# A load moved to another queue, two dummy products fewer and a new order of transposes, in the first ten microseconds of a linear-attention and SwiGLU mix

## Chip, cores, metric

One core of one Trainium2 chip. The metric is device time in microseconds (us) per execution; lower is better. "PE" is the matrix engine (TensorE), "DVE" VectorE, "ACT" ScalarE, "POOL" GpSimd, "SP" the sync engine, which here only issues loads and stores.

## The reference, cut to what matters

```python
# x: 2048 tokens of 512; all bf16
g = sigmoid((x * gate_w).sum(-1, keepdims=True))
q, k, v = split(x @ wqkv)                    # 32 heads of 16
phi = lambda t: where(t > 0, t + 1, exp(t)) + 1e-6
a = (phi(q) @ (phi(k).T @ v) / (phi(q) @ sum(phi(k)))) @ wo     # per head
b = (silu(x @ w1) * (x @ w3)) @ w2
out = g * a + (1 - g) * b
```

Only the start matters here: the keys `k = x @ wk` of the first four tiles of 128 tokens and their `phi`.

## The kernel before

A key product needs x transposed. For later tokens the load does that (DMA_TRANSPOSE in the trace; the first three landed 5.5 to 6.0 us after their issue); for the first four tiles PE transposes (four 128x128 transposes a tile into PSUM, then two copies back into `xT`, half 0 on DVE, half 1 on ACT). While nothing has landed yet, PE runs dummy products (`emit_warm`). PE's instructions are put in the order written (the kernel sets `tc.manual_schedule` for PE); on the other engines the scheduler chooses the order.

```python
    dq = nc.sync
    dq.dma_start(out=x_sb[:, 0:1, :], in_=x_r[:, 0:1, :])          # x tile 0
    for i in range(2):
        kcs = slice(2 * i, 2 * i + 2)
        nc.scalar.dma_start(out=wk_sb[:, kcs, :], in_=wqkv_r[:, kcs, D : 2 * D])
    dq.dma_start(out=x_sb[:, 1:2, :], in_=x_r[:, 1:2, :])          # x tile 1
    dq.dma_start(out=x_sb[:, 2:TPB, :], in_=x_r[:, 2:TPB, :])      # x tiles 2 and 3
    # ... (cut: all other loads, on the sync queue)
    def phi(dst, ps):                       # exp on ACT, then two operations on DVE
        e_ins = nc.scalar.activation(out=e[:], in_=ps, func=ACT.Exp)
        nc.vector.tensor_scalar(out=em[:], in0=e[:], scalar1=1.0, scalar2=1e-6, op0=ALU.min, op1=ALU.add)
        nc.vector.scalar_tensor_tensor(out=dst, in0=ps, scalar=0.0, in1=em[:], op0=ALU.max, op1=ALU.add)
    # ...
    emit_warm(6)
    def emit_xT(t):
        for h in range(2):
            # ... (cut: two transposes into PSUM)
            if h == 0:
                nc.vector.tensor_copy(out=xT_t, in_=xTp[:])
            else:
                nc.scalar.activation(out=xT_t, in_=xTp[:], func=ACT.Copy)
    def emit_k_phi(k_ps, t):
        phi(pk_sb[:, t, :], k_ps[:])
        if t == 0:
            nc.gpsimd.tensor_copy(pks[:], pk_sb[:, t, :])      # the "cast" on GpSimd
        else:
            nc.gpsimd.tensor_add(pks[:], pks[:], pk_sb[:, t, :])
    # ...
    emit_xT(0)
    emit_warm(2)
    emit_k_mm(k0[0], 0, 0); emit_k_mm(k0[0], 0, 1)
    emit_xT(1)
    emit_k_mm(k0[0], 0, 2); emit_k_mm(k0[0], 0, 3)
    emit_k_phi(k0[0], 0)
    emit_xT(2)
    for t in range(1, TPB):
        for kc in range(KC):
            emit_k_mm(k0[t], t, kc)
        emit_k_phi(k0[t], t)
        if t == 1:
            emit_xT(3)
    # ... then XP products (x^T phi(k)) alternate with the key products of tile 4 on
```

## Time and profile before

| | before |
|---|---|
| time, median of 3 (range) | 180.97 us (180.84 to 181.03) |
| the profiled execution | 181.62 us, span 179.9 us |
| PE busy | 98% of the span |
| first key product / first XP product | 4.63 / 9.67 us |
| clock step (first record of the full clock in the trace) | 6.49 us |

The profiled execution was 0.6 us slower than the timed ones. From the page of the kernel before: the span, busy time of the engines, and the shares of the chain of waits that ended last.

```profile
span 179.9 us, 2484 instructions
...
PE 176.0 (98%) x892; PEld 84.7 (47%) x892; DVE 118.9 (66%) x205; ACT 66.7 (37%) x126; POOL 61.2 (34%) x69
...
PE 96%; DVE 2%; issue 0%; DVEq 0%
```

The timeline of PE in the kernel before: start, length, engine, line, operation, count (an idle time, where there is one, stands in brackets with what ended it). The end of a PE row is modelled and runs over the start of the next; read starts.

```profile
0.84 2.72 PE L158 MATMUL warm<-const-bfloat16-1.0 128*128 128x512 bf16 x6 [0.84 <-PEq L466]
3.35 0.63 PE L169 MATMUL xTp<-ident,x_sb 128*128 128x128 bf16 x4
3.78 1.06 PE L158 MATMUL warm<-const-bfloat16-1.0 128*128 128x512 bf16 x2
4.63 1.06 PE L179 MATMUL k<-wk_sb,xT 128*128 128x512 bf16 x2
5.49 0.63 PE L169 MATMUL xTp<-ident,x_sb 128*128 128x128 bf16 x4
5.91 0.88 PE L179 MATMUL k<-wk_sb,xT 128*128 128x512 bf16 x2
6.63 0.39 PE L169 MATMUL xTp<-ident,x_sb 128*128 128x128 bf16 x4
6.86 1.03 PE L179 MATMUL k<-wk_sb,xT 128*128 128x512 bf16 x4
7.72 0.39 PE L169 MATMUL xTp<-ident,x_sb 128*128 128x128 bf16 x4
7.94 1.89 PE L179 MATMUL k<-wk_sb,xT 128*128 128x512 bf16 x8
9.67 0.38 PE L199 MATMUL XP<-pk_sb,x_sb 128*128 128x512 bf16 x1
```

There is no hole from 0.84 us on. Two dummies start at 3.78 and 4.21, two key products at 4.63 and 5.06: 0.427 us apart. That is the stream time of a product before the clock step, the time from its start to the start of the next when nothing is awaited. After the clock step eight key products take 1.73 us (7.94 to 9.67), 0.216 us each; a transpose takes 0.107 and 0.056 us.

The timeline of DVE in the kernel before, in the same stretch (its first row left out):

```profile
6.95 0.29 DVE L174 COPY xT<-xTp 128x256 bf16<-128x256 bf16 x1 [0.71 <-PE xTp L169]
7.46 0.29 DVE L139 TENSOR_SCALAR phi_m<-phi_e 128x512 bf16<-128x512 bf16 x1 [0.23 <-ACT phi_e L137]
7.79 0.69 DVE L142 SCALAR_TENSOR_TENSOR pk_sb<-k,phi_m 128x512 bf16<-128x512 f32 x1
8.40 0.28 DVE L174 COPY xT<-xTp 128x256 bf16<-128x256 bf16 x1
8.59 0.71 DVE L139 TENSOR_SCALAR phi_m<-phi_e 128x512 bf16<-128x512 bf16 x1
```

GpSimd in the kernel before, the same view:

```profile
8.54 0.61 POOL L187 CAST pks<-pk_sb 128x512 f32<-128x512 bf16 x1 [5.56 <-DVE pk_sb L142]
```

L174 is the copy of a transposed half tile, L139 the first and L142 the second DVE step of phi. The copy of tile 2 (6.95) comes ahead of the first phi step of tile 0 (7.46). The phi step of tile 1 (8.59) took 0.71 us instead of 0.29, beside GpSimd's cast (8.54 to 9.15).

### The profile page before, as it was taken

The page shows a single profiled execution, that of the slowest core. Times are in us where ns is not written, and L with a number is a line of the kernel's source. Part 1 is how long each engine was busy: PE and PEld are TensorE (multiplying, and loading weights), DVE is VectorE, ACT ScalarE, POOL GpSimd, SP SyncE. Part 2 cuts the span into 40 slices and gives each one's busy share as a digit, 9 for nine tenths or more (in the row PEclk, how much of TensorE's full clock was granted, in tenths as well). Part 3 has the DMA queues.
Part 4 walks back from the last instruction along what each step waited for, and adds up shares of the span by engine and source line. Part 5 has one row for each costly group of instructions (what it writes and reads, how often), then busy time and mean ns, then how long its engine had stood idle before and what let it go on. Part 6 is the DMA issues. An engine that isn't in the chain of part 4 may idle for free.

```text
span 179.9 us, 2484 instructions
## 1 busy us (share of the span) xinstructions
PE 176.0 (98%) x892; PEld 84.7 (47%) x892; DVE 118.9 (66%) x205; ACT 66.7 (37%) x126; POOL 61.2 (34%) x69
## 2 busy tenths in 40 slices
PE   8999999999999999999999999999999999999993
PEld 3544444474444545444445454444545444444462
DVE  1497868596998937398777374987764669776000
ACT  4443322476623324243323343333443333331221
POOL 5177665645544323254003232620032327100000
PEclk9999999999999999999999999999999999999999
DMA  6999999901005010105000101240001013300011
GB/s 191 256 253 213 287 343 378 293 13 27 9 0 99 19 47 29 44 29 113 3 4 0 44 29 44 58 89 5 0 7 47 26 55 68 63 0 0 29 51 42
DMA packets 28285, 14.88 MB, mean 83 GB/s; under 512 B 19600, under 2 KB 27248, under 8 KB 28272
## 3 DMA queue, kind: packets, MB, share of 16 engines
q1 hardware_dynamic: 27728, 14.20, 29.3%
q10 hardware_dynamic: 544, 0.52, 0.9%
q8 instruction: 7, 0.11, 0.3%
q14 instruction: 6, 0.05, 0.1%
HBM read 8.42 MB, written 2.10 MB: 58 GB/s over the span
## 4 chain that ended last, share of the span: by engine, by line
PE 96%; DVE 2%; issue 0%; DVEq 0%
PE o_ps L345 19%; PE gate_ps L302 18%; PE up_ps L308 18%; PE XP L199 8%; PE o_ps L336 8%; PE q_ps L212 8%; PE k_ps L179 6%; PE r_ps L236 3%; PE k L179 2%; PE warm L158 2%; PE o_ps L340 2%; DVE hT L318 1%; PE xTp L169 1%; DVE gs L315 1%; PE kvT_ps L406 0%; PE W_ps L433 0%
## 5 line engine op out<-in xcount | busy, mean ns | idle before, releaser
L302 PE MATMUL gate_ps<-xT,w_sb 128*128 128x512 bf16 x160 | 41.1, 379 | 0.0
L308 PE MATMUL up_ps<-xT,w_sb 128*128 128x512 bf16 x160 | 41.1, 379 | 0.0
L220 POOL TENSOR_TENSOR qz<-pq,z_sb 128x512 f32<-128x512 bf16 x16 | 18.5, 1165 | 60.6 <-DVE pq L142 58.7
L313 ACT ACTIVATE th<-gate_ps 128x512 bf16<-128x512 f32 x40 | 23.9, 597 | 38.4 <-PE gate_ps L302 38.0
L345 PE MATMUL o_ps<-w_sb,hT 128*128 128x512 bf16 (+2 forms) x180 | 37.5, 355 | 0.0
L315 DVE SCALAR_TENSOR_TENSOR gs<-th,gate_ps 128x512 bf16<-128x512 bf16 x40 | 27.3, 683 | 6.1 <-ACT th L313 5.8
L318 DVE TENSOR_TENSOR hT<-up_ps,gs 128x512 bf16<-128x512 f32 x40 | 27.6, 691 | 3.7
L139 DVE TENSOR_SCALAR phi_m<-phi_e 128x512 bf16<-128x512 bf16 x32 | 14.9, 466 | 19.6 <-ACT phi_e L137 19.6
L345 PEld LDWEIGHTS <-hT 128*128 128x128 bf16 x180 | 16.8, 97 | 17.9
L308 PEld LDWEIGHTS <-w_sb 128*128 128x128 bf16 x160 | 15.7, 98 | 18.9 <-issue 0.2
L302 PEld LDWEIGHTS <-w_sb 128*128 128x128 bf16 x160 | 15.6, 98 | 18.8 <-issue 0.3
L350 ACT ACTIVATE o_out<-o_ps,omg 128x512 bf16<-128x512 f32 (+2 forms) x17 | 11.1, 656 | 30.4 <-PE o_ps L345 30.4
L285 POOL TENSOR_TENSOR pqn<-pq,rden 128x512 bf16<-128x512 bf16 x16 | 16.6, 1055 | 14.0 <-DVE rden L278 11.7
L189 POOL TENSOR_TENSOR pks<-pks,pk_sb 128x512 f32<-128x512 f32 x15 | 17.3, 1153 | 8.9 <-DVE pk_sb L142 8.4
L223 DVE TENSOR_REDUCE den<-qz 128x32 f32<-128x512 f32 x16 | 11.0, 686 | 8.9 <-POOL qz L220 8.9
L336 PE MATMUL o_ps<-W_sb,pqT 128*128 128x512 bf16 (+2 forms) x72 | 16.8, 355 | 0.0
L212 PE MATMUL q_ps<-wq_sb,xT 128*128 128x512 bf16 x64 | 16.3, 379 | 0.0
L199 PE MATMUL XP<-pk_sb,x_sb 128*128 128x512 bf16 x64 | 16.2, 379 | 0.0
L137 ACT ACTIVATE phi_e<-k_ps 128x512 bf16<-128x512 f32 x12 | 7.2, 597 | 15.4 <-PE k_ps L179 15.4
L179 PE MATMUL k_ps<-wk_sb,xT 128*128 128x512 bf16 x48 | 12.3, 379 | 0.0
L137 ACT ACTIVATE phi_e<-q_ps 128x512 bf16<-128x512 f32 x16 | 9.6, 597 | 7.0 <-PE q_ps L212 5.8
L142 DVE SCALAR_TENSOR_TENSOR pq<-q_ps,phi_m 128x512 bf16<-128x512 f32 x16 | 11.1, 691 | 0.5
(59 smaller groups left out, 121.4 us busy)
## 6 DMA issues: line engine op xcount, KB each, us to landing
w_sb<-in_B_w_dram SPq DMA_DIRECT2D x3, 1280.0 KB, 11.4
out_dram<-o_out SPq DMA_DIRECT2D x15, 128.0 KB, 1.7
x_sb<-in_A_x_dram SPq DMA_DIRECT2D x3, 512.0 KB, 4.5
wk_sb<-in_A_wqkv_dram ACTq DMA_DIRECT2D x2, 256.0 KB, 3.4
wq_sb<-in_A_wqkv_dram SPq DMA_DIRECT2D x1, 512.0 KB, 5.4
wv_sb<-in_A_wqkv_dram SPq DMA_DIRECT2D x1, 512.0 KB, 6.2
wo_sb<-in_A_wo_dram SPq DMA_DIRECT2D x1, 512.0 KB, 12.4
x_sb<-in_A_x_dram SPq DMA_DIRECT2D x2, 128.0 KB, 2.7
```

Of the source, the lines that this page charges most:

```text
L179: nc.tensor.matmul(k_ps[:], lhsT=xT[:, kc, t * P : (t + 1) * P], rhs=wk_sb[:, kc, :], start=(kc == 0), stop=(kc == KC - 1),)
L189: nc.gpsimd.tensor_add(pks[:], pks[:], pk_sb[:, t, :])
L199: nc.tensor.matmul(XP_ps[dc][:], lhsT=x_sb[:, t, dc * P : (dc + 1) * P], rhs=pk_sb[:, t, :], start=(t == 0), stop=(t == NT - 1),)
L212: nc.tensor.matmul(q_ps[:], lhsT=xT[:, kc, ts_tok], rhs=wq_sb[:, kc, :], start=(kc == 0), stop=(kc == KC - 1),)
L220: nc.gpsimd.tensor_tensor(out=qz[:], in0=st[tb, "pq"][:, tt, :], in1=z_sb[:], op=ALU.mult)
L302: nc.tensor.matmul(gate_ps[:], lhsT=w1_sb[:, kc, fsl], rhs=xT[:, kc, tok_sl], start=(kc == 0), stop=(kc == KC - 1),)
L308: nc.tensor.matmul(up_ps[:], lhsT=w3_sb[:, kc, fsl], rhs=xT[:, kc, tok_sl], start=(kc == 0), stop=(kc == KC - 1),)
L313: nc.scalar.activation(out=th[:], in_=gate_ps[:], func=ACT.Tanh, scale=0.5)
L315: nc.vector.scalar_tensor_tensor(out=gs[:], in0=th[:], scalar=1.0, in1=gate_ps[:], op0=ALU.add, op1=ALU.mult)
L318: nc.vector.tensor_tensor(out=st[tb, "hT"][:, fc, :], in0=up_ps[:], in1=gs[:], op=ALU.mult)
L336: nc.tensor.matmul(o_ps[:], lhsT=st[tb, "pqT"][:, c, tsl], rhs=W_sb[:, c, a:b], start=(c == 0), stop=False,)
L345: nc.tensor.matmul(o_ps[:], lhsT=st[tb, "hT"][:, fc, tsl], rhs=w2_sb[:, fc, a:b], start=False, stop=(fc == FC - 1),)
```

## The change

Its intent: bring the second half of wk in earlier, take out dummy products that seemed too many, and put each later group of transposes between the second and third product of the key tile before it, so that the copies have time.

```diff
-    for i in range(2):
-        kcs = slice(2 * i, 2 * i + 2)
-        nc.scalar.dma_start(out=wk_sb[:, kcs, :], in_=wqkv_r[:, kcs, D : 2 * D])
+    nc.scalar.dma_start(out=wk_sb[:, 0:2, :], in_=wqkv_r[:, 0:2, D : 2 * D])
+    dq.dma_start(out=wk_sb[:, 2:4, :], in_=wqkv_r[:, 2:4, D : 2 * D])
     dq.dma_start(out=x_sb[:, 1:2, :], in_=x_r[:, 1:2, :])
@@
-    emit_warm(6)
+    emit_warm(5)
@@
     emit_xT(0)
-    emit_warm(2)
-    (first key tile, transposes of tile 2, loop over the other tiles: as above)
+    emit_warm(1)
+    for t in range(TPB):
         for kc in range(KC):
+            if kc == KC // 2 and t + 1 < TPB:
+                emit_xT(t + 1)
             emit_k_mm(k0[t], t, kc)
         emit_k_phi(k0[t], t)
-        if t == 1:
-            emit_xT(3)
```

(The removed lines in brackets are cut; the kernel before has them above.) What the diff doesn't say: the scheduler also turned DVE's order round. After, the first phi step of tile 0 stands ahead of the copy of tile 2, and that of tile 1 ahead of the copy of tile 3.

More of the change, by code (lines that the diff above doesn't have):

```diff
@@ L364 @@
     emit_xT(0)
-    emit_warm(2)
-    emit_k_mm(k0[0], 0, 0)
-    emit_k_mm(k0[0], 0, 1)
-    emit_xT(1)
-    emit_k_mm(k0[0], 0, 2)
-    emit_k_mm(k0[0], 0, 3)
-    emit_k_phi(k0[0], 0)
-    emit_xT(2)
-    for t in range(1, TPB):
+    emit_warm(1)
+    for t in range(TPB):
         for kc in range(KC):
+            if kc == KC // 2 and t + 1 < TPB:
+                emit_xT(t + 1)
             emit_k_mm(k0[t], t, kc)
         emit_k_phi(k0[t], t)
-        if t == 1:
-            emit_xT(3)
     XP_ps = [psX.tile([P, D], FP32, tag=f"XP{dc}", name=f"XP{dc}") for dc in range(KC)]
```

## The prediction

> What bounds the kernel. The page gives PE 98% busy in a span of 179.9 us; 96% of the chain that ended last is PE. In the timeline PE runs back to back from the first dummy product at 0.84 us; after 6.9 us I find only about 0.4 us of PE gaps, none of them a wait for a load. So only the first 10 us, and the number of PE instructions in them, can move the time, and a shift of the first XP product (L199, at 9.67 us) should reach the end almost unchanged.
>
> The granted clock rises at 6.49 us. Before it 128x512 products follow each other every 427 ns and transposes every 107 ns; after it every 216 and 55 ns. [...]I assume that the step stays near 6.5 us.
>
> What changes.
> 1. One dummy fewer in front. x tile 0 lands at 3.21 us; its weight load starts at 3.25, the first transpose at 3.35, exactly 427 ns after the sixth dummy. The load held it as much as the dummy did: gain 0 to 0.07 us, and a hole of about 0.4 us in PE.
> 2. One dummy fewer behind. The first key product moves from 4.63 to about 4.2 us (it then waits for the DVE copy of xT, which ends at 4.10, not for wk). That is 427 ns of slow clock, but the clock step doesn't move with it: what is really won is one product at the fast clock, about 0.22 us.
> 3. Loads. In the trace they land: wk first half 3.85, x tile 1 4.21, wk second half 4.97, x tiles 2-3 5.88 us. On the other queue the second half should land at about 4.4 (needed at 5.5 now), x tile 1 at 4.6 to 4.9 (needed at 5.05), x tiles 2-3 near 5.9 (needed at 6.8). No new wait; also nothing that was waited for before.
> 4. The order on DVE changes, by the instruction orders: before, the copy of xT tile 2 stood ahead of phi_m of k0; now phi_m of k0 stands ahead of it, and phi_m of k1 ahead of the copy of tile 3. That phi_m waits for k0's last product and ACT's exp: last product at about 5.91, ends 6.54, exp (0.60) to 7.17, phi_m (0.29) to 7.49, copy (0.28) to about 7.73, weight load, product k2 at about 7.83. PE would be ready at 7.50: a new wait of about 0.33 us. The same at tile 3: about 0.06 us; if GpSimd's cast, which coincides with a phi_m of 0.71 instead of 0.29 us in the trace, gets in first, 0.5 us.
>
> Sum: -0.24 + 0.33 + 0.06, about +0.1 us: the first XP product at about 9.8 us instead of 9.67. All of it lies on the critical path.
>
> Predicted: 181.1 us, range 180.6 to 181.7. Faster by over 2%: 0.005; within 2%: 0.99; slower by over 2%: 0.005.
>
> What would show it: first key product at 4.2 us; no PE wait for x or wk; the first k2 product waiting 0.2 to 0.5 us for DVE's xT copy, which follows phi_m of k0; clock step near 6.5 us; first XP product at 9.7 to 9.9; from there the same lengths as before.
>
> What would make it wrong: the clock step moving ([...]an earlier step gains); x tile 1 landing after 5.1; the copies not waiting behind phi_m, then 180.7; phi_m of k1 delayed by GpSimd, then 181.6.

Two passages are cut from it, both on what moves the clock step. -0.24 + 0.33 + 0.06 = +0.15 us, which the prediction rounds to about +0.1 us.

## The result

| | before | after |
|---|---|---|
| time, median (range) | 181.03 us (180.84 to 181.74), 6 runs | 181.88 us (181.26 to 182.11), 6 runs |
| profiled execution: time, span | 181.62, 179.9 us | 181.69, 180.0 us |
| clock step | 6.49 us | 4.16 us |
| first key product / first XP product | 4.63 / 9.67 us | 4.34 / 9.86 us |
| first XP product to the end | 170.24 us | 170.10 us |

The ratio is 1.0033 (95% interval 1.0009 to 1.0058): slower by about 0.6 us. A ratio is the mean time of one kernel's runs over that of the other's of the same rounds, so not quite the ratio of the medians. A second set of the same two kernels gave 1.0001 (0.9980 to 1.0021), see below.

From the page of the kernel after, the lines that answer to those of before:

```profile
span 180.0 us, 2480 instructions
...
PE 174.9 (97%) x890; PEld 83.4 (46%) x890; DVE 118.7 (66%) x205; ACT 66.8 (37%) x126; POOL 61.2 (34%) x69
...
PE 93%; DVE 3%; DMA 2%; SPq 0%; ACT 0%; issue 0%; DVEq 0%
```

The timeline of PE after:

```profile
0.84 2.29 PE L157 MATMUL warm<-const-bfloat16-1.0 128*128 128x512 bf16 x5 [0.84 <-PEq L458]
3.56 0.61 PE L168 MATMUL xTp<-ident,x_sb 128*128 128x128 bf16 x4 [0.42 <-DMA x_sb<-in_A_x_dram]
3.96 0.48 PE L157 MATMUL warm<-const-bfloat16-1.0 128*128 128x512 bf16 x1
4.34 0.60 PE L178 MATMUL k<-wk_sb,xT 128*128 128x512 bf16 x2
5.32 0.40 PE L168 MATMUL xTp<-ident,x_sb 128*128 128x128 bf16 x4 [0.38 <-DMA x_sb<-in_A_x_dram]
5.56 1.04 PE L178 MATMUL k<-wk_sb,xT 128*128 128x512 bf16 x4
6.57 0.40 PE L168 MATMUL xTp<-ident,x_sb 128*128 128x128 bf16 x4
6.80 1.17 PE L178 MATMUL k<-wk_sb,xT 128*128 128x512 bf16 x4
7.81 0.39 PE L168 MATMUL xTp<-ident,x_sb 128*128 128x128 bf16 x4
8.03 0.59 PE L178 MATMUL k<-wk_sb,xT 128*128 128x512 bf16 x2
8.99 1.04 PE L178 MATMUL k<-wk_sb,xT 128*128 128x512 bf16 x4 [0.36 <-DVE xT L173]
9.86 0.38 PE L198 MATMUL XP<-pk_sb,x_sb 128*128 128x512 bf16 x1
```

The clock had stepped up at 4.16 us, 2.3 us earlier than in the trace before, and still the first XP product started later. PE waited for x tile 0 (row at 3.56), for x tile 1 (5.32), and for a DVE copy (8.99). A bracket shows only the time in which the modelled end of the row before had passed, and not all waits have one. Measured from start to start against the stream time of a product, the waits are 0.63, 0.54 and 0.52 us, with smaller ones in front of the first key product (DVE copy, 0.07), at 6.57 (x tiles 2 and 3, 0.13) and in front of the first product of key tile 2 (inside the row of 6.80; DVE copy, 0.13). The timeline of DVE after:

```profile
6.82 0.29 DVE L138 TENSOR_SCALAR phi_m<-phi_e 128x512 bf16<-128x512 bf16 x1 [0.88 <-ACT phi_e L136]
7.03 0.28 DVE L173 COPY xT<-xTp 128x256 bf16<-128x256 bf16 x1
7.23 0.68 DVE L141 SCALAR_TENSOR_TENSOR pk_sb<-k,phi_m 128x512 bf16<-128x512 f32 x1
8.07 0.66 DVE L138 TENSOR_SCALAR phi_m<-phi_e 128x512 bf16<-128x512 bf16 x1 [0.16 <-ACT phi_e L136]
8.65 0.28 DVE L173 COPY xT<-xTp 128x256 bf16<-128x256 bf16 x1
```

GpSimd in the kernel after, the same view:

```profile
7.97 0.61 POOL L186 CAST pks<-pk_sb 128x512 f32<-128x512 bf16 x1 [4.99 <-DVE pk_sb L141]
```

L173 is the copy now, L138 the first phi step. The copies of tiles 2 and 3 (7.03, 8.65) each follow a phi step (6.82, 8.07). The second of these took 0.66 us; the cast had begun at 7.97, 0.09 us before it. The chain of waits after (start, length, what) passes through exactly this:

```profile
1.72 3.56 DMA x_sb<-in_A_x_dram
...
7.44 0.60 ACT phi_e L136
...
8.07 0.66 DVE phi_m L138
8.73 0.21 DVE xT L173
...
8.99 1.04 PE k L178 x4
```

### How the traces are compared when the clock steps at a different time in each

The step came at 6.49 us in one trace and 4.16 in the other, so their first XP products can't be compared as they are. Up to the step a product costs twice as much (0.427 against 0.216 us); so each us that the step comes later costs about half a us, which is an estimate from these two times. I therefore use "first XP product minus half the step". Over all traces (all times in us; "load" and "DVE" are PE's waits up to the first XP product, start to start against stream time, holes of over 25 ns, by what the trace says ended them):

| kernel | step | first XP | first XP - step/2 | load | DVE |
|---|---|---|---|---|---|
| before | 6.49 | 9.67 | 6.43 | 0 | 0 |
| before, again | 5.68 | 9.27 | 6.44 | 0 | 0 |
| after | 4.16 | 9.86 | 7.78 | 1.30 | 0.72 |
| after, again | 6.83 | 10.28 | 6.86 | 0.50 | 0.62 |
| only the loads | 6.76 | 9.80 | 6.43 | 0 | 0 |
| only the dummies | 6.91 | 9.69 | 6.24 | 0.57 | 0 |
| only the order | 6.52 | 10.00 | 6.74 | 0 | 0.29 |
| after, copies first | 5.29 | 8.90 | 6.26 | 0.40 | 0.03 |
| after, no cast | 4.34 | 9.75 | 7.58 | 1.49 | 0.28 |
| copies first, old loads | 7.04 | 9.87 | 6.34 | 0.63 | 0 |
| copies first, split loads | 5.92 | 9.34 | 6.38 | 0.70 | 0.03 |

The two traces of before, with steps 0.8 us apart, agree within 0.01 us: the measure works where nothing is awaited. It flatters a kernel with a late step a little: a wait in the slow time costs only half of itself, because the products that it displaces are made up at twice the speed after the step (an estimate from the same two times).

In the 14 traces the step lies between 3.49 and 7.04 us, that is 2.7 to 6.2 us after the first product (0.84 us). In the three long warm-ups below it came 2.7, 5.6 and 5.7 us after it, and the 24 dummies followed each other without a hole: at 0.427 us up to the step and 0.216 us after it they fill the time to the first transposes (8.87, 7.36 and 8.79 us). So the step spreads almost as widely without holes. No run tested what sets the step.

### The profile page after: what moved, and what is told of

Same layout as the page of the kernel before. It is cut to its first block, busy times and chain, and to the rows that moved or that the text cites. A ratio compares the mean times of both kernels' runs of the same rounds, so it can differ in the third digit from the quotient of the medians.

```text
span 180.0 us, 2480 instructions
## 1 busy us (share of the span) xinstructions
PE 174.9 (97%) x890; PEld 83.4 (46%) x890; DVE 118.7 (66%) x205; ACT 66.8 (37%) x126; POOL 61.2 (34%) x69
## 4 chain that ended last, share of the span: by engine, by line
PE 93%; DVE 3%; DMA 2%; SPq 0%; ACT 0%; issue 0%; DVEq 0%
PE o_ps L344 19%; PE gate_ps L301 18%; PE up_ps L307 18%; PE o_ps L335 8%; PE XP L198 8%; PE q_ps L211 8%; PE k_ps L178 6%; PE r_ps L235 3%; DMA x_sb<-in_A_x_dram 2%; PE o_ps L339 2%; PE k L178 1%; DVE hT L317 1%; DVE gs L314 1%; PE kvT_ps L398 0%; PE W_ps L425 0%; DVE rden L276 0%
## 5 line engine op out<-in xcount | busy, mean ns | idle before, releaser
L138 DVE TENSOR_SCALAR phi_m<-phi_e 128x512 bf16<-128x512 bf16 x32 | 14.6, 457 | 21.7 <-ACT phi_e L136 21.6
```

## The experiments

Three theories. **O**: DVE takes phi steps ahead of the xT copies, and PE waits for the copies. **L**: on the new queue x tile 1 and x tiles 2 and 3 land later, and PE waits for them. **D**: fewer dummies leave a hole in PE that delays the clock step; this was a guess, which no trace had shown. The experiments ran in three sets of four, each set on one chip, beside 11 runs of before on that chip. All kernels gave correct results.

### Only the loads

```diff
 (kernel before)
+    nc.scalar.dma_start(... first half of wk); dq.dma_start(... second half of wk)   # instead of both on scalar
```

> The kernel before with only the second half of wk moved to the sync queue behind x tile 0. Theory L (loads): x tile 1 now stands behind 256 KB on its own queue and lands at 5.0 to 5.3 us instead of 4.21, as in the trace after; PE waits 0.2 to 0.8 us in front of the transposes of x tile 1 (more the earlier the clock steps up); time +0.2 to +0.6 us. Theory O (order on DVE): no new PE wait of over 0.1 us, time within 0.15 us of before. Theory D (fewer dummies, hole in PE): the same, no change. The first XP product shows it beside the clock step.

Measured: 1.0003 (0.9981 to 1.0024). x tile 1 landed at 5.12 us (4.21 before), as L says, but PE did not wait, so L's expected wait and time were missed: with the clock step at 6.76 us the old order starts the transposes of tile 1 only at 5.49 us, as before. So the later landing is real and was harmless in this trace. An execution with an early step was not caught in a trace.

### Only the dummies

```diff
 (kernel before)
-    emit_warm(6)
+    emit_warm(5)
@@
-    emit_warm(2)
+    emit_warm(1)
```

> The kernel before with 5 and 1 dummy products instead of 6 and 2, all else as before. Theory D: the hole of about 0.4 us that a missing front dummy leaves delays the clock step, so that it comes at 6.5 us or later, and the time rises by 0.3 us or more. Theories O and L: nothing is lost; the front dummy only becomes idle time until x tile 0 lands, the rear one gives 0 to 0.4 us; time -0.3 to 0.0 us.

Measured: 0.9994 (0.9974 to 1.0014). The step came at 6.91 us; first XP minus half the step fell by 0.19 us. The two dummies are worth 2 x 0.216 = 0.43 us; 0.57 us of load waits appeared (0.16 for x tile 0 and 0.41 for the second half of wk, which landed at 5.57), all in the slow time and so counting half: -0.43 + 0.28 = -0.15. D is out as a cause of the 0.3 us or more that it claims: the interval ends 0.25 us above before, and the steps of the two groups overlap. The kernels with 5 and 1 dummies had steps from 4.16 to 7.04 us, those with 6 and 2 from 5.68 to 6.76.

### Only the order

```diff
 (kernel before: same loads, 6 and 2 dummies)
+    for t in range(TPB):          # the loop of the change
```

> The kernel before with only the new order of transposes and key products (loads on the old queues, 6 and 2 dummies). Theory O: DVE takes phi_m of tile t ahead of the copy of xT tile t+2, so PE waits 0.1 to 0.4 us before the first product of key tile 2 and 0.3 to 0.7 us before that of tile 3, where phi_m sits beside GpSimd's cast and takes 0.66 to 0.71 us instead of 0.29; time +0.4 to +0.8 us. Theories L and D: no such waits, time within 0.15 us of before.

Measured: 1.0015 (0.9995 to 1.0035). One DVE wait, 0.29 us before key tile 2 (as O expected), and none before tile 3 (O expected 0.3 to 0.7 us); first XP minus half the step +0.31 us. Less than expected, because here the phi step of tile 1 won against the cast. DVE of this kernel in the timeline (L139 phi step, L174 copy):

```profile
7.48 0.29 DVE L139 TENSOR_SCALAR phi_m<-phi_e 128x512 bf16<-128x512 bf16 x1 [1.24 <-ACT phi_e L137]
7.68 0.28 DVE L174 COPY xT<-xTp 128x256 bf16<-128x256 bf16 x1
...
8.56 0.29 DVE L139 TENSOR_SCALAR phi_m<-phi_e 128x512 bf16<-128x512 bf16 x1
8.78 0.29 DVE L174 COPY xT<-xTp 128x256 bf16<-128x256 bf16 x1
```

And its GpSimd:

```profile
8.63 0.69 POOL L187 CAST pks<-pk_sb 128x512 f32<-128x512 bf16 x1 [5.64 <-DVE pk_sb L142]
```

The phi step began at 8.56 and took 0.29 us; the cast began at 8.63, after it.

### After, with the copies first

```diff
 (kernel after; DVE in the order written)
+    with tc.manual_schedule(engines={ENG.DVE}):
+        (loop as after, but emit_k_phi(k0[t-1], t-1) follows emit_xT(t+1))
```

> The changed kernel with the order on DVE put back: xT copies of tiles 2 and 3 ahead of phi_m of tiles 0 and 1, the order on PE as changed. Theory O: the waits in front of key tiles 2 and 3 (0.13 and 0.52 us in the trace after) fall under 0.1 us each; time 0.4 to 0.6 us below the changed kernel, about that of before. Theory L: the wait for x tile 1 (0.4 us or more) stays and the time stays 0.3 to 0.6 us above before. If both hold, half of the loss is left.

Measured: 0.9998 (0.9976 to 1.0021), mean 181.23 us beside 181.22 of before. DVE waits fell from 0.72 and 0.62 us to 0.03. The wait for x tile 1 stayed (0.32 us). First XP minus half the step: 6.26, below that of before by 0.17 and below the late-step trace of after by 0.60. O is confirmed on the trace; on the time it is not, since the two sets of after (1.0033 and 1.0001) differ by as much as O claims. L's wait is confirmed too, but not its price: the time did not stay 0.3 to 0.6 us above before. PE of this kernel in the timeline:

```profile
5.00 0.51 PE L168 MATMUL xTp<-ident,x_sb 128*128 128x128 bf16 x4
...
7.57 1.50 PE L178 MATMUL k<-wk_sb,xT 128*128 128x512 bf16 x6
8.90 1.03 PE L198 MATMUL XP<-pk_sb,x_sb 128*128 128x512 bf16 x4
```

The transposes of tile 1 start at 5.00 us, right after the landing (4.96); the six products at 7.57 (the last two of key tile 2 and all of tile 3) run through to the first XP product, where after had its wait of 0.52 us.

### After, again

No edit.

> The changed kernel once more, for its time and for a second trace with another clock step. All theories: the ratio to before again lies at 1.002 to 1.005. Theory O: waits of together 0.3 to 0.9 us in front of key tiles 2 and 3, released by DVE's xT copy. Theory L: a wait for x tile 1 of 0.1 us or more, less the later the clock steps up. First XP product near 0.84 + PE work at the fast clock 5.64 + waits + half of the slow time.

Measured: 1.0001 (0.9980 to 1.0021), six runs from 180.88 to 182.09 us. The expected ratio missed. The trace fell on the slowest of the six: step 6.83 us, load waits 0.37 (x tile 0) and 0.13 (x tile 1), DVE waits 0.10 and 0.52. Its DVE and GpSimd show the same pair as the first trace of after, the cast 0.12 us ahead of the phi step:

```profile
8.39 0.61 POOL L186 CAST pks<-pk_sb 128x512 f32<-128x512 bf16 x1 [5.40 <-DVE pk_sb L141]
...
8.52 0.63 DVE L138 TENSOR_SCALAR phi_m<-phi_e 128x512 bf16<-128x512 bf16 x1 [0.19 <-ACT phi_e L136]
...
9.07 0.28 DVE L173 COPY xT<-xTp 128x256 bf16<-128x256 bf16 x1
...
9.41 1.04 PE L178 MATMUL k<-wk_sb,xT 128*128 128x512 bf16 x4 [0.36 <-DVE xT L173]
```

This trace gives the sum at a step nearly that of before (6.83 and 6.49 us). It is bookkeeping: it shows that no wait is overlooked, not what causes each. Two dummies less: -0.43. Load waits 0.50, all before the step and so half: +0.25. DVE waits: +0.62. Together +0.44 us; first XP minus half the step is +0.43 (6.86 against 6.43).

### A long warm-up: before, after, and after with copies first

```diff
 (each of the three kernels)
-    emit_warm(6)      # or 5
+    emit_warm(24)
@@
-    emit_warm(1)      # in the two changed ones
+    emit_warm(2)
```

With the clock fast and all early loads landed before the first transpose, only order is left: in the three traces the first transposes started at 8.87, 7.36 and 8.79 us, after the clock step of each, and in no trace of this case did x tiles 2 and 3 land after 6.78 us.

> The kernel before with 24 instead of 6 dummies in front: when the transposes start, the clock is fast and all early loads have landed. Only the order can matter then. All theories: from the first transpose to the first XP product 4.8 to 5.0 us (16 transposes at 56, 18 products at 216 ns, next to no waits). Total time 2 to 3 us longer than before.

> The changed kernel with 24 dummies in front and 2 (as before) behind the first transposes. Theory O: the same work takes 0.4 to 0.9 us longer than in the long-warm kernel before (5.2 to 5.8 us from the first transpose to the first XP product), in waits before key tiles 2 and 3 for DVE. Theory L and D: no difference to it of over 0.15 us, as no load is awaited and the clock is fast.

> The same with the xT copies put ahead of phi_m on DVE, as in the kernel before; the order on PE stays as changed. Theory O: within 0.15 us of the long-warm kernel before (4.8 to 5.0 us). A rival, that it is the new order on PE itself and not that on DVE: 0.4 us or more longer.

Measured, from the first transpose to the first XP product: 4.79, 5.12 and 4.86 us, with DVE waits (holes of over 25 ns) of 0, 0.28 and 0.03 us. So the order on PE alone costs almost nothing (0.07 us) and the order on DVE 0.26 us. That is below O's range of 0.4 to 0.9 us, as the phi step of tile 1 again won against the cast (11.05 against 11.10 us). The total times (185.08, 184.43 and 185.11 us, two runs each, ratios 1.0216, 1.0181, 1.0218) follow the clock step (6.58, 3.49 and 6.42 us), through the number of dummies at the slow clock, and say nothing about the order; before was also longer than I had expected.

### After, without the cast

```diff
 (kernel after)
-        if t == 0:
-            nc.gpsimd.tensor_copy(pks[:], pk_sb[:, t, :])
-        else:
+        if t == 1:
+            nc.gpsimd.tensor_add(pks[:], pk_sb[:, 0, :], pk_sb[:, 1, :])
+        elif t > 1:
```

> The changed kernel without GpSimd's cast of the first tile: its first work is now the sum of tiles 0 and 1. Theory O with the race: the 0.52 us in front of key tile 3, seen twice where the cast began 0.09 to 0.12 us ahead of phi_m of tile 1 and that phi_m took 0.63 to 0.66 us, falls below 0.15 us, and that phi_m takes about 0.29 us; the wait in front of key tile 2 (0.10 to 0.13) stays. Time about 0.3 us below the changed kernel. If the cast has nothing to do with it, the 0.5 us stay.

Measured: 1.0006 (0.9986 to 1.0026). The phi step of tile 1 took 0.29 us, as said:

```profile
8.32 0.29 DVE L138 TENSOR_SCALAR phi_m<-phi_e 128x512 bf16<-128x512 bf16 x1 [0.28 <-ACT phi_e L136]
```

The wait before key tile 3 fell from 0.52 to 0.28 us, not below 0.15; the one before tile 2 vanished. With the cast 0.05 to 0.12 us ahead the phi step took 0.63 to 0.71 us and ended 0.15 us after the cast (before, after, after again); with the phi step 0.07 us ahead (only the order) or no cast it took 0.29. The time can't decide it, as the two sets of after differ by more. As I read the trace, the reason is in the loads: x tiles 2 and 3 landed at 6.78 us and PE waited 0.45 us for them, which gave DVE time for the copy of tile 2 but delayed the end of key tile 1, so the full distance between exp, phi step and copy showed at tile 3 instead. The distance is paid once, at one tile or the other (0.28 to 0.29 us in the three traces where the phi step of tile 1 took 0.29 us); a cast that comes first adds 0.3 us (0.62 and 0.65 us at both tiles together in the two traces of after).

### Copies first, with the old loads

```diff
 (after with copies first)
-    nc.scalar.dma_start(... first half of wk); dq.dma_start(... second half of wk)
+    (both halves on scalar, as before)
```

> The new order on PE and 5 and 1 dummies, with the loads as before and the xT copies ahead of phi_m. Theory L: x tile 1 lands at 4.2 to 4.3 us again and its wait (0.13 to 0.54 us) is gone; but the second half of wk lands at 5.0 to 5.7 us and may now be awaited by 0 to 0.4 us. No DVE wait over 0.1 us. Time 0 to 0.3 us below before.

Measured: 1.0018 (0.9999 to 1.0038). x tile 1 landed at 4.59 us and was not awaited, the second half of wk at 5.33, not awaited either (the step came late, 7.04 us). x tile 0 landed at 3.50 and was awaited for 0.63 us in the hole that the front dummy left. First XP minus half the step: 6.34, 0.09 below before; the time was not below.

### Copies first, with split loads

```diff
 (after with copies first)
-    dq.dma_start(out=x_sb[:, 1:2, :], in_=x_r[:, 1:2, :])
+    nc.scalar.dma_start(out=x_sb[:, 1:2, :], in_=x_r[:, 1:2, :])
```

> As after with copies first, but x tile 1 on the scalar queue behind wk's first half, and wk's second half on the sync queue behind x tile 0. Theory L: it is the place in the queue that counts; x tile 1 lands at 4.3 to 4.7 us instead of 5.0 to 5.3, wk's second half at 4.7 to 5.0; the wait for x tile 1 falls below 0.15 us. Time 0.1 to 0.4 us below before. If a load's landing depended on the bytes alone, x tile 1 would land at 5.0 or later again.

Measured: 1.0018 (0.9995 to 1.0042). x tile 1 landed at 5.26 us, not at 4.3 to 4.7, and was awaited for 0.30 us; the second half of wk landed at 5.02. L, in the form that the bytes ahead in a load's own queue decide, missed: with 384 KB ahead (x tile 0 and half of wk) x tile 1 landed at 5.13 us in the mean, with 256 KB ahead on the other queue no earlier, and the time was not below before. It landed as the rival named in the expectation says (the bytes alone decide: 5.0 us or later), which in one trace is a hint and no proof: up to the landing of x tile 1 both queues together had moved 0.75 MB in before (at 4.21 us), 0.99 MB in after (5.28) and 1.06 MB here (`--dma` with a window up to the landing). Whatever the queues, the later of x tile 1 and wk's second half landed at 4.96 to 5.72 us in all 14 traces; which of the two it was changed with the queues. In this run the second queue brought no earlier landing (5.26 us, against 5.13 in the mean).

### Before, against itself

No edit.

> The kernel before against itself: a second trace with another clock step, and what the interval is worth. All theories: ratio 0.998 to 1.002. From the traces: first XP product near 0.84 + PE work at the fast clock 6.07 + half of the time to the clock step, plus waits; with a step under 5 us waits for loads should appear here too, with a step over 6 us none.

Measured: 0.9990 (0.9970 to 1.0011). Two identical kernels differ by 0.001; that is the size of most differences above. No load wait with a step at 5.68 us.

## Why the prediction was right, and where not

The range held (the ratio of 1.0033 is 181.6 us on the 180.97 quoted), and so did "within 2%" and the sign. The centre was low: +0.1 us predicted, +0.6 and +0.02 us measured in the two sets (1.0033 and 1.0001 of 181 us), +0.3 in the mean. Part of this is luck. The median of the six runs, 181.88 us, lies above the range, beside 181.03 for before in the same rounds. And the first XP product came at 9.86 us, inside the 9.7 to 9.9 that I had named, only because two misses cancelled: the earlier clock step is worth -1.17 us, and the waits, less the dummies, cost +1.35 us. Point by point:

1. *What bounds the kernel: PE, only the first 10 us can move it, and a shift of the first XP product reaches the end.* Right, with a small error: from the first XP product to the end the time fell from 170.24 to 170.10 us, because one wait of PE for phi of the last key tile (0.13 us) was gone.
2. *The clock step stays near 6.5 us.* Wrong as an assumption: 4.16 and 6.83 us in two traces of after. There was a hint: the profiled execution of before (181.62 us) was 0.6 us slower than its timed ones, which fits a late step.
3. *One front dummy is worth 0 to 0.07 us and leaves a hole of about 0.4 us.* The hole is there: 0.63 and 0.37 us for x tile 0. *One rear dummy is worth about 0.22 us.* What each is worth was not taken apart; both together were worth 0.43 less half the load waits (dummies alone, 0.19 us measured).
4. *"No new wait" from the loads.* **This step failed.** I had x tile 1 landing at 4.6 to 4.9 us and x tiles 2 and 3 near 5.9. With the new loads they landed at 4.96 to 5.29 and 5.99 to 6.78 us (means of seven traces 5.13 and 6.43; with the old loads, six traces, 4.36 and 5.98). Both orders need x tile 1 ahead of the second half of wk, since the transposes of tile 1 stand before the third key product in both; the change brought the half of wk forward (mean 5.30 to 4.79) at the cost of x tile 1. In the traces of after x tile 1 was awaited for 0.13 us at the late step, in the slow time, and for 0.54 us at the early one.
5. *DVE's order gives a new wait of 0.33 us before key tile 2 and 0.06 before tile 3, or 0.5 there if the cast gets in first.* The mechanism was right: undoing it took the DVE waits from 0.6 to 0.7 us down to 0.03. The sizes were off: 0.13 and 0.10 at tile 2; at tile 3 the case that I had put second came true, 0.52 twice, so the two waits came to 0.62 and 0.65 us instead of 0.39. The race is decided by 0.05 to 0.12 us (cast first by 0.09 and 0.12 us in after, phi step first by 0.07 with only the order and by 0.05 after the long warm-up), so it could not be called from the trace of before.
6. *Sum +0.1* (the terms add to +0.15). With the steps allowed for it is +0.43 at the first XP product (after again) and, with point 1, about +0.3 at the end. Of the missing 0.28 us, 0.23 are point 5: with the cast first the wait at tile 3 was 0.46 us larger than in the sum, and the one at tile 2 was 0.23 us smaller. The rest, about 0.05 us, is the load waits less what the dummies gave.

Not settled: the gain or loss in time beyond "between 0 and 0.6 us slower", since the two sets of after differ by as much and their intervals reach from -0.4 to +1.05 us; whether before would also wait for its loads when the step comes at 4 us, for which no trace was caught, so that the large load waits of after at an early step (1.30 us) are not all to be charged to the change; and why x tile 0 landed anywhere from 2.92 to 3.53 us whatever the kernel. On the second an estimate can be made: with the step at 4.16 us and the stream times above, PE in before would be ready for x tiles 2 and 3 at about 5.5 us, and with the old loads they landed at 5.81 to 6.13 us. If the loads land the same at an early step, before would lose 0.3 to 0.6 us there, nearly as much as after lost to x tiles 1 to 3 (0.67 us). No version was shown to beat before: with the copies first the trace says 0.17 us less at equal step, the time says 0.9998 with 0.2% to either side.

## What to carry to other kernels

When work on PE is reordered, look at the order on the engines that feed it: here a copy for PE had slipped behind a step of a slow chain on DVE, and behind a GpSimd cast beside which that step took 0.63 to 0.71 us instead of 0.29. When a load is brought forward, name the one that is put back, and ask which of the two the new order needs first. And before comparing the starts of two traces, line up their clock steps: the first XP products of two traces of the same kernel lay 0.40 us (before) and 0.42 us (after) apart, as much as this change is worth.
